# Sparse attention and a gated FFN: block transposes on VectorE, with transfers between partitions, in place of TensorE transposes after the first block

## The chip, the cores and the metric

The kernel runs on one core of one Trainium2 chip. The metric is the device time of one execution in microseconds, as the median of several runs. A hardware profile of one such execution is shown below. Engines: PE is TensorE (PEld its weight loads), ACT is ScalarE, DVE is VectorE, POOL is GpSimd, and SP is SyncE, which issues all DMAs of this kernel.

## What is computed

```python
B, H, S, D = 8, 8, 576, 64
scores = q @ k.transpose(0, 1, 3, 2) / np.sqrt(D)
rel = pos[:, None] - pos[None, :]
mask_local   = (rel >= 0) & (rel < 32)                         # heads 0 to 3
mask_strided = (rel >= 0) & (pos[None, :] % 32 == pos[:, None] % 32)   # heads 4 to 7
attn = softmax(np.where(mask, scores, -1e9))
x = (attn @ v).transpose(0, 2, 1, 3).reshape(4608, 512)
h = x @ w_in                       # 512 -> 2048
out = (h * sigmoid(h)) @ w_out     # 2048 -> 512
```

All arrays are float32. The masks make the attention sparse: a local head needs, for 32 queries, 64 keys; a strided head needs, for each of 32 residues, the 18 positions of that residue.

## The kernel before

**FFN.** The 4608 tokens are worked through in 9 blocks of 512 tokens. A block has 16 chunks `fc` of 128 of the 2048 hidden channels. For a chunk, `hidden` (L525) makes 12 matmuls of 128x512, then `silu` makes the gated value from it (tanh on ACT at L535; the product at L539, the rounded high half at L547 and the low half at L551, all on DVE), and `output` (L571) makes 12 matmuls of 128x512 with the chunk before (`lag`). Each factor is split into a high and a low float32r half, and three products of halves stand for one. When a block is done, `store` copies the four output banks `po` to `osb` on ACT (L579; two `osb` buffers) and sends them to memory (L581).

**Attention.** Heads go in pairs on the 128 partitions. For one batch of 576 tokens there are six groups: three local ones (12 tiles of 32 queries each) and three strided ones (8, 8 and 6 tiles of three residues, 54 queries each). A group passes these steps:

- `scores` (L384): small matmuls into two PSUM banks; `peak` (L402 on DVE, L408 on ACT): masking, row maximum and exponential, into the tile `sm`; `total` (L428, L429) and, for strided groups, `scale` (L432).
- `turn` (L438): one 128x128 PE transpose for each 128 columns of `sm`, three or four in a group; `turned` (L442): ACT copies the bank to `pt`.
- `values` (L455 local, L460 strided): `pt` times V. A strided result is copied by ACT to the token tile `xb` (`sorted`, L484). A local one is divided on DVE (`share`, L471) into `xq`, turned back by three PE transposes (`back`, L491) and copied by ACT to `xb` (`done`, L496).
- `x_high` (ACT, L513) and `x_low` (DVE, L517) split `xb` into the FFN's input halves `xhi` and `xlo`.

**Order.** The first batch, and the first block of the FFN, are put in order by a planner (`Steps`) with a cost for each step. From block 1 to block 6 the attention of one batch is laid into one FFN block by hand: `between` is called after the `output` of each chunk, and at the chunks 0, 3, 5, 8, 11 and 13 of a block it issues a **burst**: `turn` of group c+1, `back` of c-1, `values` of c, `scores` and `total` of c+2. Local and strided groups alternate: the bursts at 0, 5 and 11 have a local group c, and those at 3, 8 and 13 a strided one. There are 36 bursts. The order on PE is that of the code; the order on the other engines after block 0, SP's among them, comes out of the tile framework's scheduler. Four PSUM banks (`ps`) are taken in turn by `hidden` and by all attention steps, and the other four are `po`.

Of the kernel before, what the change touches and what calls it, by code (L numbers as in the profile page):

```python
# [13 lines left out]
F32 = mybir.dt.float32  # L14
# [11 lines left out]
STRIDE = 32  # L26
NJ = S // STRIDE
NP = H // 2
P = 128
# [10 lines left out]

KW = 64
SEQ = 3 * NJ
QW = 448
VT = 12
KBUFS = 2
VBUFS = 2
KFIRST = 4
VFIRST = 6  # L50
XBUFS = NP + 2


AHEAD = 6
# [3 lines left out]
class Group:  # L58
    def __init__(self, local, first, count):
        self.local, self.first, self.count = local, first, count  # L60
        self.rows = STRIDE if local else KW
        self.per = P // self.rows
        self.n = count // self.per
        step = STRIDE if local else SEQ
        self.q0 = [step * t for t in range(count)]
        half = S // STRIDE
        gap = [STRIDE if local and first < half <= first + t else 0 for t in range(count)]
        self.k0 = [q0 + g for q0, g in zip(self.q0, gap)]
        self.nq = self.q0[-1] + self.rows
        self.nk = self.k0[-1] + KW  # L70

        self.starts = [
            tuple(t % self.per for t in range(c * self.per, (c + 1) * self.per)
                  if local and (first + t) % half == 0)
            for c in range(self.n)
        ]

# [3 lines left out]
NG = len(GROUPS)  # L81
# [112 lines left out]
def sparse_attention_ffn(ctx: ExitStack, tc: tile.TileContext, kqt, vt, w_in, w_out, out):  # L194
    nc = tc.nc
# [3 lines left out]
    att = ctx.enter_context(tc.tile_pool(name="att", bufs=2))  # L199
# [31 lines left out]
    def keep(m, p0, rows, shape, steps, base, channel):  # L231
        part = m[p0 : p0 + rows, : math.prod(shape)]
        nc.gpsimd.affine_select(
            out=part, in_=part, pattern=[[s, c] for s, c in zip(steps, shape)],
            base=base, channel_multiplier=channel, compare_op=ALU.is_ge, fill=NEG,
        )

    masks = {}
    m = mask("mask_local")
    for t in range(P // STRIDE):  # L240
        keep(m, t * STRIDE, STRIDE, [KW], [1], -1, -1)
        keep(m, t * STRIDE, STRIDE, [KW], [-1], STRIDE, 1)
    masks[True, ()] = m
    for starts in sorted({s for g in GROUPS for s in g.starts if s}):
        first = const.tile([P, 72], F32, name="mask_first" + "".join(map(str, starts)))
        nc.gpsimd.tensor_copy(out=first, in_=m)
        for t in starts:
            keep(first, t * STRIDE, STRIDE, [KW], [1], -STRIDE, 0)
        masks[True, starts] = first
    m = mask("mask_strided")  # L250
    for t in range(P // KW):
        keep(m, t * KW, KW, [4, NJ], [-NJ, -1], 0, 1)
        keep(m, t * KW, KW, [4, NJ], [NJ, 0], NJ - 1, -1)
    masks[False, ()] = m
    const.tile([P, 96], F32, name="pad1")

# [35 lines left out]
    copy = {"DVE": nc.vector.tensor_copy, "ACT": nc.scalar.copy}  # L292
# [55 lines left out]
    def place_of(b):  # L348
        if b not in xs:
            xs[b] = xp.tile([P, NP, S], F32, name="xb")  # L350
        return xs[b]

    class Attention:


        def __init__(self, b, at):
            self.b, self.at, self.gi = b, at, order_of(b)[at]
            self.g = g = GROUPS[self.gi]
            self.kbd, self.vbd = kbds[kbd_of(b, at)], vbds[vbd_of(b, at)]
            self.cols = g.n * P  # L360
            self.tiles = [
                (t, t // g.per, slice(t % g.per * g.rows, (t % g.per + 1) * g.rows))
                for t in range(g.count)
            ]

            self.quick = NG * b + at < 2 * NG + 2
# [11 lines left out]
        def scores(self):  # L378
            g, kbd = self.g, self.kbd
            self.pss = [self.bank("pss") for _ in range(2)]  # L380
            for t, c, rows in self.tiles:
                for h in range(2):
                    at = slice(h * D, (h + 1) * D)
                    nc.tensor.matmul(  # L384
                        self.pss[h][rows, c * KW : (c + 1) * KW],
                        kbd[at, 1, g.q0[t] : g.q0[t] + g.rows],
                        kbd[at, 0, g.k0[t] : g.k0[t] + KW], start=True, stop=True,
                    )
# [33 lines left out]
        def total(self):  # L422
            rsum = self.rsum
            if self.quick:
                nc.vector.tensor_reduce(
                    out=rsum, in_=self.s_sb, op=ALU.add, axis=mybir.AxisListType.X
                )
            nc.vector.tensor_scalar_add(rsum, rsum, 1e-9)  # L428
            nc.vector.reciprocal(rsum, rsum)  # L429
# [4 lines left out]
        def turn(self):  # L434
            self.psp = self.bank("psp")
            for c in range(self.g.n):
                at = slice(c * P, (c + 1) * P)
                nc.tensor.transpose(self.psp[:, at], self.sm[:, at], ident)  # L438

        def turned(self, engine="ACT"):  # L440
            self.pt = att.tile([P, 512], F32, name="pt")
            copy[engine](out=self.pt[:, : self.cols], in_=self.psp[:, : self.cols])  # L442

        def values(self):
            g, pt, vbd = self.g, self.pt, self.vbd
            if g.local:
                self.pso = [self.bank("pso") for _ in range(2)]
            else:
                self.pso = self.bank("pso")
            for t, c, rows in self.tiles:  # L450
                p0 = c * P + rows.start
                for h in range(2):
                    at = slice(h * KW, (h + 1) * KW)
                    if g.local:
                        nc.tensor.matmul(  # L455
                            self.pso[h][rows, c * D : (c + 1) * D],
                            pt[at, p0 : p0 + g.rows], vbd[at, t], start=True, stop=True,
                        )
                    else:
                        nc.tensor.matmul(  # L460
                            self.pso[h * D : (h + 1) * D, t * SEQ : (t + 1) * SEQ], vbd[at, t],
                            pt[at, p0 : p0 + SEQ], start=True, stop=True,
                        )

        def share(self):
            g = self.g
            self.xq = att.tile([P, 3 * P], F32, name="xq", bufs=1)
            o_sb = self.xq.rearrange("p (c h d) -> p c h d", h=2, d=D)[:, : g.n]
            for h, o_ps in enumerate(self.halves(self.pso)):
                inv = self.rsum[:, :, h].unsqueeze(2).broadcast_to([P, g.n, D])  # L470
                nc.vector.tensor_mul(o_sb[:, :, h], o_ps, inv)  # L471
# [15 lines left out]
        def back(self):  # L487
            self.psx = self.bank("psp")
            for c in range(self.g.n):
                at = slice(c * P, (c + 1) * P)  # L490
                nc.tensor.transpose(self.psx[:, at], self.xq[:, at], ident)  # L491

        def done(self, engine="ACT"):
            flat = place_of(self.b).rearrange("p n s -> p (n s)")
            x0 = self.g.first * STRIDE
            copy[engine](out=flat[:, x0 : x0 + self.cols], in_=self.psx[:, : self.cols])  # L496

    def new_x():
        return [[None] * NP for _ in range(2)]
# [83 lines left out]
    groups = [Attention(b, at) for b in range(B) for at in range(NG)]  # L583
# [160 lines left out]
    scored, weighed = set(range(2 * NG + 2)), set(range(2 * NG))  # L744

    def load_due():

        while due:
            kind, j = due[0]
            bufs, load_one, read = (KBUFS, load_qk, scored) if kind == "k" else (  # L750
                VBUFS, load_v, weighed)
            if j - bufs not in read:
                return
            load_one(groups[j])
            due.pop(0)

    def scores(c):  # L760
        if c < len(groups):
            groups[c].scores()
            scored.add(c)
            load_due()
            groups[c].peak()

    def total(c):
        if c < len(groups):
            groups[c].total()
            if not groups[c].g.local:  # L770
                groups[c].scale()

    def turn(c):
        if c < len(groups):
            groups[c].turn()
            groups[c].turned()

    def values(c):
        if c < len(groups):
            groups[c].values()  # L780
            weighed.add(c)
            load_due()
            (groups[c].share if groups[c].g.local else groups[c].sorted)()

    def back(c):
        if groups[c].g.local:
            groups[c].back()
            groups[c].done()

    plan = {}  # L790
    for c in range(2 * NG, len(groups)):
        b, at = divmod(c, NG)
        plan[b - 1, (0, 3, 5, 8, 11, 13)[at]] = c

    def between(k, fc):
        if (k, fc) in plan:
            c = plan[k, fc]
            turn(c + 1)
            back(c - 1)
            values(c)  # L800
            scores(c + 2)
            total(c + 2)

    load_due()
    lag = (0, NFC - 1, state["g", NFC - 1])
    po = state["po"]
# [82 lines left out]
```

## Time and profile before

| | us |
|---|---|
| median of 3 runs | 921.07 (920.71 to 922.52) |
| profiled execution | 923.33 |
| its span | 921.5 (1.8 outside the span) |
| PE busy | 904.5 (98%) |
| DVE busy | 436.6 (47%) |
| ACT busy | 315.1 (34%) |
| DMA, mean throughput | 68 GB/s |
| granted PE clock, mean | 0.998 |

The span falls into three parts. Up to about 144 us the first batch's attention, the weights and block 0 are worked on; from 144 to about 744 us six blocks of 100 us each hold the 36 bursts; the last two blocks hold only FFN, with 16 chunks of 24 matmuls. A busy PE says little by itself, since its matmuls overlap: two matmuls of 128x512 that follow each other start 0.227 us apart, while each is recorded with 0.39 us. What a step costs PE is therefore read from the distance of the starts.

### The profile page before, as it was taken

How to read it: one execution, taken by the hardware profiler on the slowest of the kernel's cores; microseconds unless marked ns; L12 is line 12 of the kernel's file. 1: busy time of each engine (PE TensorE's matmuls, PEld its weight loads, DVE VectorE, ACT ScalarE, POOL GpSimd, SP SyncE). 2: the span in 40 equal slices, each digit the busy share in tenths (PEclk: the TensorE clock that was granted, in tenths of full speed). 3: DMA queues.
4: the chain of work that ended last, by engine and by line, in shares of the span. 5: the costliest groups of instructions: out<-in, count | busy, mean ns of one | idle time of the engine just before them, and what ended most of it. 6: DMA issues, size and time to landing. Idle time of an engine off the chain costs nothing.

```text
span 921.5 us, 18028 instructions
## 1 busy us (share of the span) xinstructions
PE 904.5 (98%) x7451; PEld 742.9 (81%) x7451; DVE 436.6 (47%) x1408; ACT 315.1 (34%) x897; POOL 19.0 (2%) x38
## 2 busy tenths in 40 slices
PE   8999998999999999999999999999999999999997
PEld 6777776888888888888888888888888888888886
DVE  6999665434534444434444353444443333333332
ACT  3877453422532243224342252234332221112112
POOL 4100000000000000000000000000000000000000
PEclk9999999999999999999999999999999999999999
DMA  9674533201301102112220131120210010001001
GB/s 336 217 244 155 161 101 102 64 29 38 114 27 41 63 32 91 54 29 69 83 63 30 39 101 40 37 66 32 87 40 9 1 46 1 1 1 46 1 1 46
DMA packets 34962, 63.04 MB, mean 68 GB/s; under 512 B 2624, under 2 KB 22080, under 8 KB 34880
## 3 DMA queue, kind: packets, MB, share of 16 engines
q1 hardware_dynamic: 34880, 61.89, 20.3%
q8 instruction: 58, 0.95, 0.4%
q14 instruction: 24, 0.20, 0.1%
HBM read 52.45 MB, written 9.44 MB: 67 GB/s over the span
## 4 chain that ended last, share of the span: by engine, by line
PE 87%; DVE 7%; DMA 3%; ACT 2%; issue 0%; ACTq 0%; SPq 0%
PE ps L525 39%; PE po L571 39%; PE ps L384 3%; PE ps L460 2%; DMA stage<-w_in 2%; PE ps L438 1%; PE ps L455 1%; DVE stage L287 1%; DVE w L327 1%; DVE glo L551 1%; DVE sm L402 1%; PE ps L491 1%; DMA stage<-w_out 1%; DVE th L539 1%; PE ps L639 1%; ACT stage L276 1%
## 5 line engine op out<-in xcount | busy, mean ns | idle before, releaser
L525 PE MATMUL ps<-xhi,w 128*128 128x512 f32 x1152 | 386.6, 395 | 2.2 <-DVE th L539 1.5
L525 PEld LDWEIGHTS ps<-xhi,w 128*128 128x128 f32 x1152 | 216.2, 188 | 50.5 <-DVE th L539 1.9
L539 DVE SCALAR_TENSOR_TENSOR th<-th,ps 128x512 f32<-128x512 f32 (+1 forms) x147 | 99.3, 675 | 319.2 <-ACT th L535 319.1
L535 ACT ACTIVATE th<-ps 128x512 f32<-128x512 f32 (+1 forms) x147 | 86.3, 587 | 430.0 <-PE ps L525 427.7
L525 PE MATMUL ps<-xlo,w 128*128 128x512 f32 x576 | 225.2, 391 | 1.7 <-DVE xlo L517 1.7
L571 PE MATMUL po<-w,ghi 128*128 128x512 f32 x504 | 155.4, 390 | 0.7 <-ACT ghi L547 0.7
L525 PEld LDWEIGHTS ps<-xlo,w 128*128 128x128 f32 x576 | 108.2, 188 | 23.8 <-DVE xlo L517 3.0
L571 PEld LDWEIGHTS po<-w,ghi 128*128 128x128 f32 x504 | 94.4, 188 | 20.4 <-ACT ghi L547 0.8
L551 DVE TENSOR_TENSOR glo<-th,ghi 128x512 fp32r<-128x512 f32 (+1 forms) x147 | 100.3, 682 | 12.2 <-ACT ghi L547 1.6
L571 PE MATMUL po<-w,glo 128*128 128x512 f32 x252 | 98.3, 390 | 0.3 <-DVE glo L551 0.3
L571 PE MATMUL po<-stage,ghi 128*128 128x512 f32 x288 | 88.7, 389 | 0.0
L408 ACT ACTIVATE sm<-sm,sums 128x64 f32<-128x64 f32 x226 | 75.5, 336 | 13.2 <-DVE sums L402 12.6
L571 PE MATMUL po<-v,ghi 128*128 128x512 f32 x216 | 66.7, 390 | 0.0
L571 PEld LDWEIGHTS po<-stage,ghi 128*128 128x128 f32 x288 | 54.1, 188 | 11.3
L547 DVE CAST ghi<-th 128x512 fp32r<-128x512 f32 (+1 forms) x137 | 57.7, 421 | 10.4
L571 PEld LDWEIGHTS po<-w,glo 128*128 128x128 f32 x252 | 47.3, 188 | 11.0 <-DVE glo L551 1.2
L571 PE MATMUL po<-stage,glo 128*128 128x512 f32 x144 | 56.1, 389 | 0.0
L442 ACT COPY pt<-ps 128x384 f32<-128x384 f32 (+1 forms) x40 | 20.6, 514 | 79.8 <-PE ps L438 79.8
L571 PEld LDWEIGHTS po<-v,ghi 128*128 128x128 f32 x216 | 40.4, 188 | 8.5 <-ACT ghi L547 0.2
L571 PE MATMUL po<-k,ghi 128*128 128x512 f32 x144 | 44.3, 389 | 0.0
L571 PE MATMUL po<-v,glo 128*128 128x512 f32 x108 | 42.2, 391 | 0.4 <-DVE glo L551 0.4
L408 ACT ACTIVATION_READ_ACCUMULATOR sm<-sm,sums 128x1 f32 x226 | 42.6, 188 | 0.0
(77 smaller groups left out, 737.1 us busy)
## 6 DMA issues: line engine op xcount, KB each, us to landing
v<-vt SPq DMA_DIRECT2D x24, 384.0 KB, 3.6
out<-osb SPq DMA_DIRECT2D x36, 256.0 KB, 2.0
stage<-w_in SPq DMA_DIRECT2D x16, 512.0 KB, 4.8
stage<-w_out SPq DMA_DIRECT2D x16, 512.0 KB, 3.6
k<-kqt SPq DMA_DIRECT2D x16, 442.0 KB, 4.0
k<-kqt SPq DMA_DIRECT2D x16, 416.0 KB, 4.6
v<-vt SPq DMA_DIRECT2D x16, 256.0 KB, 2.8
k<-kqt SPq DMA_DIRECT2D x8, 448.0 KB, 4.2
```

Source lines behind the costliest of these rows:

```text
L276: nc.scalar.activation(out=value, in_=value, func=AF.Prelu, scale=2.0**-112, alpha=-(2.0**32))
L287: nc.vector.scalar_tensor_tensor(out=upper, in0=upper, scalar=3, in1=lower, op0=ALU.logical_shift_left, op1=ALU.bitwise_or,)
L384: nc.tensor.matmul(self.pss[h][rows, c * KW : (c + 1) * KW], kbd[at, 1, g.q0[t] : g.q0[t] + g.rows], kbd[at, 0, g.k0[t] : g.k0[t] + KW], s ...
L408: nc.scalar.activation(out=s_sb[:, c, h], in_=s_sb[:, c, h], func=AF.Exp, bias=peaks[:, c, h : h + 1], scale=-1.0, accum_out=rsum[:, c, h ...
L442: copy[engine](out=self.pt[:, : self.cols], in_=self.psp[:, : self.cols])
L460: nc.tensor.matmul(self.pso[h * D : (h + 1) * D, t * SEQ : (t + 1) * SEQ], vbd[at, t], pt[at, p0 : p0 + SEQ], start=True, stop=True,)
L525: nc.tensor.matmul(ph, weight(0, wi, fc)[:, cc * P : (cc + 1) * P], x[xi][cc], start=(cc, n) == (0, 0), stop=(cc, n) == (NP - 1, 2),)
L535: nc.scalar.activation(out=th[:, cols], in_=ph[:, cols], func=AF.Tanh, scale=0.5)
L539: nc.vector.scalar_tensor_tensor(out=th[:, cols], in0=th[:, cols], scalar=1.0, in1=ph[:, cols], op0=ALU.add, op1=ALU.mult,)
L547: copy[engine](out=g[0][:, cols], in_=th[:, cols])
L551: nc.vector.tensor_sub(out=g[1][:, cols], in0=th[:, cols], in1=g[0][:, cols].bitcast(F32))
L571: nc.tensor.matmul(po[tt], g[gi][:, cols], weight(1, wi, fc), start=fc == 0 and n == 0, stop=fc == NFC - 1 and n == 2,)
```

## The change

After block 0 no group is turned by PE any more. `turn_by_blocks` follows `scale` (or `total`) in the same burst as the scores: one VectorE instruction transposes each 32x32 block of `sm` where it lies, into another `sm` buffer, and 16 DMAs from SP then move the 16 parts (32 partitions by 96 or 128 columns) to the partitions where `pt` needs them. `back_by_blocks` does the same from `xq` to `xb`, right after `share`, so that `back` and `done` are gone too. Group 13, whose scores belong to block 0, is turned this way between block 0 and block 1; group 12 is still turned on PE by the planner. The 128 rows of a bank are dealt to tiles in another order (`at`), so strided queries lie as two halves of 27 in 32 columns each, and the strided loads of q and k have up to 512 columns in place of 442. `xq` gets two buffers, the `sm` ring stays at three, and the `xhi` and `xlo` rings go from 6 to 5.

```diff
-QW = 448
+QW = 512
+HALF = SEQ // 2
-XBUFS = NP + 2
+XBUFS = NP + 1
...
+        self.at = [(t % self.n, t // self.n) for t in range(count)]
...
+        def blocks(self, name, bufs, src, dst):
+            n, size = self.g.n, P // STRIDE
+            mid = att.tile([P, 512 if name == "sm" else 3 * P], F32, name=name, bufs=bufs)
+            mid = mid[:, : self.cols]
+            nc.vector.transpose(
+                out=mid.rearrange("p (j c q) -> p c j q", j=size, q=STRIDE),
+                in_=src.rearrange("p (c j k) -> p c j k", j=size, k=STRIDE),
+            )
+            part = n * STRIDE
+            for r, j in itertools.product(range(size), range(size)):
+                nc.sync.dma_start(
+                    out=dst[j * STRIDE : (j + 1) * STRIDE, r * part : (r + 1) * part],
+                    in_=mid[r * STRIDE : (r + 1) * STRIDE, j * part : (j + 1) * part],
+                )
+
+        def turn_by_blocks(self):
+            pt = att.tile([P, 512], F32, name="pt")[:, : self.cols]
+            self.blocks("sm", 3, self.sm[:, : self.cols], pt)
+            self.pt = pt.rearrange("k (r c q) -> k c r q", r=P // STRIDE, q=STRIDE)
+
+        def back_by_blocks(self):
+            flat = place_of(self.b).rearrange("p n s -> p (n s)")
+            x0 = self.g.first * STRIDE
+            self.blocks("xq", 2, self.xq, flat[:, x0 : x0 + self.cols])
...
-                            pt[at, p0 : p0 + SEQ], start=True, stop=True,
+                            pt[at, c, r : r + 2, :HALF], start=True, stop=True,
...
-            self.xq = att.tile([P, 3 * P], F32, name="xq", bufs=1)
+            self.xq = att.tile([P, 3 * P], F32, name="xq", bufs=2)
...
     def scores(c):
         if c < len(groups):
             groups[c].scores()
             scored.add(c)
             load_due()
             groups[c].peak()
-
-    def total(c):
-        if c < len(groups):
             groups[c].total()
             if not groups[c].g.local:
                 groups[c].scale()
-
-    def turn(c):
-        if c < len(groups):
-            groups[c].turn()
-            groups[c].turned()
+            groups[c].turn_by_blocks()
 
     def values(c):
-        if c < len(groups):
-            groups[c].values()
-            weighed.add(c)
-            load_due()
-            (groups[c].share if groups[c].g.local else groups[c].sorted)()
-
-    def back(c):
+        groups[c].values()
+        weighed.add(c)
+        load_due()
         if groups[c].g.local:
-            groups[c].back()
-            groups[c].done()
+            groups[c].share()
+            groups[c].back_by_blocks()
+        else:
+            groups[c].sorted()
...
     def between(k, fc):
         if (k, fc) in plan:
-            c = plan[k, fc]
-            turn(c + 1)
-            back(c - 1)
-            values(c)
-            scores(c + 2)
-            total(c + 2)
-
+            values(plan[k, fc])
+            scores(plan[k, fc] + 2)
+
+    groups[2 * NG + 1].turn_by_blocks()
     load_due()
```

On PE, a strided burst (chunk 3 or 8) before, from the last matmul of `output` to the first of `hidden`:

```order
L571 MATMUL po<-w_0_701,glo 128x512
L438 MATMUL ps<-ident,sm 128x128 x3
L491 MATMUL ps<-ident,xq 128x128 x3
L460 MATMUL ps<-pt,v_77 64x54 x16
L384 MATMUL ps<-k_81 64x64 x12
L525 MATMUL ps<-xhi,w_0_616 128x512
```

The six transposes at its start are those of the groups c+1 and c-1. In the changed kernel a local burst (chunk 0, 5 or 11) begins directly with `values` (now L486), and its first eight matmuls stand so:

```order
L486 MATMUL ps<-v_77,pt 32x64 [waits DMAHW5_49,DMAHW7_49,DMAHW0_49,PE_49]
L486 MATMUL ps<-v_77,pt 32x64 [waits DMAHW2_49,DMAHW1_49]
L486 MATMUL ps<-v_77,pt 32x64 x4
L486 MATMUL ps<-v_77,pt 32x64 [waits DMAHW4_49,DMAHW3_49]
L486 MATMUL ps<-v_77,pt 32x64 [waits DMAHW6_49,DMAHW5_49]
```

The names DMAHW0 to DMAHW7 are the eight semaphores that SP's DMAs take in turn. No transpose is left, and of each six matmuls the first two wait for two transfers each (eight of the 24 do, in the places 1, 2, 7, 8, 13, 14, 19 and 20). One row here is two matmul records in the trace.

On ACT, at the end of a block (from chunk 0's tanh on, blocks 2 to 6) before:

```order
L535 ACTIVATE th<-ps 128x512 [waits DVE_49,PE_49]
L579 ACTIVATE osb<-po 128x512 [waits DMAHW0_49,PE_49]
L579 ACTIVATE osb<-po 128x512 [waits DMAHW1_49,PE_49]
L442 COPY pt<-ps 128x512 [waits PE_49]
L579 ACTIVATE osb<-po 128x512 [waits DMAHW6_49,Activation_49]
L579 ACTIVATE osb<-po 128x512 [waits DMAHW7_49,Activation_49]
L408 ACTIVATE sm,sums<-sm,sums 128x64 [waits DVE_49] x6
L535 ACTIVATE th<-ps 128x512 [waits PE_49] x2
```

and at the same place now:

```order
L570 ACTIVATE th<-ps 128x512 [waits DVE_49,PE_49]
L614 ACTIVATE osb<-po 128x512 [waits PE_49] x2
L411 ACTIVATE sm,sums<-sm,sums 128x64 [waits DVE_49,Activation_49]
L411 ACTIVATE sm,sums<-sm,sums 128x64 [waits DVE_49] x5
L570 ACTIVATE th<-ps 128x512 [waits PE_49]
L614 ACTIVATE osb<-po 128x512 [waits DMAHW5_49,Activation_49]
L614 ACTIVATE osb<-po 128x512 [waits DMAHW6_49,Activation_49]
L570 ACTIVATE th<-ps 128x512 [waits PE_49]
```

The third and fourth copy of the finished block's output banks have moved behind the six exponentials of the burst and behind chunk 1's tanh.

On SP, at the same place now (before, no transfer but those of `osb`, V, k and q stood here):

```order
L616 DMA out<-osb 128x512 [waits DMAHW5_49,Activation_49]
L616 DMA out<-osb 128x512 [waits DMAHW6_49,Activation_49]
L348 DMA v_77<-vt 128x768 [waits DMAHW7_49,PE_49]
L344 DMA k_81<-kqt 128x1024 [waits DMAHW0_49]
L460 DMA xb<-xq 32x96 [waits DMAHW1_49,DVE_49]
L616 DMA out<-osb 128x512 [waits DMAHW2_49,Activation_49]
L460 DMA xb<-xq 32x96 [waits DMAHW3_49]
L616 DMA out<-osb 128x512 [waits DMAHW4_49,Activation_49]
```

Fourteen more transfers from `xq` to `xb` and the sixteen from `sm` to `pt` follow. Each DMA waits for the one issued eight places ahead of it, and fourteen of the transfers to `xb` now stand behind the stores.

More of the change, by code (lines that the diff above doesn't have):

```diff
@@ L63, in __init__ @@
         self.n = count // self.per
-        step = STRIDE if local else SEQ
-        self.q0 = [step * t for t in range(count)]
+        self.q0 = [self.rows * t for t in range(count)]
         half = S // STRIDE
         gap = [STRIDE if local and first < half <= first + t else 0 for t in range(count)]
-        self.k0 = [q0 + g for q0, g in zip(self.q0, gap)]
+        self.k0 = [(STRIDE if local else SEQ) * t + g for t, g in enumerate(gap)]
         self.nq = self.q0[-1] + self.rows
         self.nk = self.k0[-1] + KW
+        self.at = [(t % self.n, t // self.n) for t in range(count)]
         self.starts = [
-            tuple(t % self.per for t in range(c * self.per, (c + 1) * self.per)
-                  if local and (first + t) % half == 0)
+            tuple(r for t, (at, r) in enumerate(self.at)
+                  if at == c and local and (first + t) % half == 0)
             for c in range(self.n)
@@ L250, in sparse_attention_ffn @@
     m = mask("mask_strided")
-    for t in range(P // KW):
-        keep(m, t * KW, KW, [4, NJ], [-NJ, -1], 0, 1)
-        keep(m, t * KW, KW, [4, NJ], [NJ, 0], NJ - 1, -1)
+    for t in range(P // STRIDE):
+        q0 = t % 2 * HALF
+        keep(m, t * STRIDE, STRIDE, [4, NJ], [-NJ, -1], q0, 1)
+        keep(m, t * STRIDE, STRIDE, [4, NJ], [NJ, 0], NJ - 1 - q0, -1)
     masks[False, ()] = m
@@ L361, in __init__ @@
             self.tiles = [
-                (t, t // g.per, slice(t % g.per * g.rows, (t % g.per + 1) * g.rows))
-                for t in range(g.count)
+                (t, c, slice(r * g.rows, (r + 1) * g.rows)) for t, (c, r) in enumerate(g.at)
             ]
@@ L440, in turned @@
         def turned(self, engine="ACT"):
-            self.pt = att.tile([P, 512], F32, name="pt")
-            copy[engine](out=self.pt[:, : self.cols], in_=self.psp[:, : self.cols])
+            pt = att.tile([P, 512], F32, name="pt")
+            copy[engine](out=pt[:, : self.cols], in_=self.psp[:, : self.cols])
+            self.pt = pt[:, : self.cols].rearrange("k (c r q) -> k c r q", r=P // STRIDE, q=STRIDE)
+        def blocks(self, name, bufs, src, dst):
[20 more added lines that the diff above has]
+            self.blocks("xq", 2, self.xq, flat[:, x0 : x0 + self.cols])
         def values(self):
@@ L450, in values @@
             for t, c, rows in self.tiles:
-                p0 = c * P + rows.start
+                r = rows.start // STRIDE
                 for h in range(2):
@@ L456, in values @@
                             self.pso[h][rows, c * D : (c + 1) * D],
-                            pt[at, p0 : p0 + g.rows], vbd[at, t], start=True, stop=True,
+                            pt[at, c, r], vbd[at, t], start=True, stop=True,
                         )
@@ L495, in done @@
             x0 = self.g.first * STRIDE
-            copy[engine](out=flat[:, x0 : x0 + self.cols], in_=self.psx[:, : self.cols])
+            dst = flat[:, x0 : x0 + self.cols].rearrange(
+                "p (r c q) -> p c r q", c=self.g.n, q=STRIDE
+            )
+            src = self.psx[:, : self.cols].rearrange("p (c r q) -> p c r q", c=self.g.n, q=STRIDE)
+            copy[engine](out=dst, in_=src)
     def new_x():
@@ L851 @@
             for i in range(STRIDE if g.local else SEQ):
-                q_from[gi, g.q0[t] + i] = place(g.local, g.first + t, i)
+                at = i if g.local else i // HALF * STRIDE + i % HALF
+                q_from[gi, g.q0[t] + at] = place(g.local, g.first + t, i)
             for i in range(KW if g.local else SEQ):
```

## The prediction, made before the changed kernel ran

> **What bounds the kernel now.** I read the page first: the busy shares, and the chain of work that ended last with its shares by engine.
>
> ```profile
> span 921.5 us, 18028 instructions
> PE 904.5 (98%) x7451; PEld 742.9 (81%) x7451; DVE 436.6 (47%) x1408; ACT 315.1 (34%) x897; POOL 19.0 (2%) x38
> PE 87%; DVE 7%; DMA 3%; ACT 2%; issue 0%; ACTq 0%; SPq 0%
> ```
>
> Then busy time by stage: start and end in us, length, busy time of PE, PEld, DVE, ACT and POOL (instructions in brackets), granted PE clock, DMA share, GB/s.
>
> ```profile
> 0.00:144.00 144.00, 134.02 (x1515) 105.88 (x1516) 114.97 (x391) 84.54 (x154) 19.01 (x38) 0.99 0.59 197
> 344.00:444.00 100.00, 100.00 (x879) 82.79 (x878) 44.05 (x157) 34.79 (x122) 0.00 (x0) 1.00 0.18 56
> ```
>
> A block of the middle part has PE busy for all of its 100 us at full clock; VectorE and ScalarE are idle for more than half of it, and the DMA engines work a fifth of it. So in that part what leaves PE shortens the time, and what VectorE and DMA gain is paid only where PE comes to wait for it. The FFN's matmuls stay; the change can act only in the 36 bursts, at the block ends and in the first 144 us. What it takes from PE is seen in the groups of instructions from 141 to 741 us (count, busy time, mean ns of one, idle before):
>
> ```profile
> L438 PE MATMUL ps<-ident,sm 128*128 128x128 f32 x117 | 18.4, 271 | 1.8 <-DVE sm L432 1.8
> L491 PE MATMUL ps<-ident,xq 128*128 128x128 f32 x54 | 8.8, 272 | 0.0
> ```
>
> That is 171 transposes. Their 271 ns overlap, so I priced them from the weight loads' starts, on the timeline of one strided burst:
>
> ```profile
> 364.34 0.19 PEld L571 LDWEIGHTS po<-w,glo 128*128 128x128 f32 x1
> 364.56 0.48 PEld L438 LDWEIGHTS ps<-ident,sm 128*128 128x128 f32 x3
> 365.01 0.36 PEld L491 LDWEIGHTS ps<-ident,xq 128*128 128x128 f32 x3
> 365.53 0.95 PEld L460 LDWEIGHTS ps<-pt,v 64*64 64x64 f32 x30 [0.17 <-issue]
> 367.08 0.19 PEld L525 LDWEIGHTS ps<-xhi,w 128*128 128x128 f32 x1
> ```
>
> one local burst, and one whose group has three transposes (last row):
>
> ```profile
> 377.64 0.19 PEld L571 LDWEIGHTS po<-w,glo 128*128 128x128 f32 x1
> 378.62 0.56 PEld L455 LDWEIGHTS ps<-v,pt 64*32 64x32 f32 x48 [0.17 <-PE ps L438]
> 379.12 0.80 PEld L384 LDWEIGHTS ps<-k 64*32 64x32 f32 x48
> 380.01 0.19 PEld L525 LDWEIGHTS ps<-xhi,w 128*128 128x128 f32 x1
> 416.05 0.69 PEld L384 LDWEIGHTS ps<-k 64*32 64x32 f32 x48
> ```
>
> and the same turns from FFN to small tiles in block 0, where no transposes stand between:
>
> ```profile
> 59.82 0.19 PEld L571 LDWEIGHTS po<-w,glo 128*128 128x128 f32 x1
> 60.36 0.56 PEld L455 LDWEIGHTS ps<-v,pt 64*32 64x32 f32 x48 [0.35 <-issue]
> 119.58 0.19 PEld L525 LDWEIGHTS ps<-xhi,w 128*128 128x128 f32 x1
> 120.13 0.78 PEld L460 LDWEIGHTS ps<-pt,v 64*64 64x64 f32 x24 [0.36 <-issue]
> ```
>
> **The change, term by term.**
>
> (a) *Transposes gone.* From the last FFN load to `values` takes 365.53 - 364.34 = 1.19 us with six transposes, 378.62 - 377.64 = 0.98 with four, 0.54 and 0.55 with none. So six are worth 0.65 and four 0.44: 0.109 us each, and the switch to small tiles stays. 171 x 0.109 = **-18.6 us**.
>
> By the Trainium skill's page "VectorE: DVE Perf Modes", section "The three transpose paths", a 128x128 transpose of bf16 takes 390 ns on TensorE and 311 ns on VectorE, and its "Rules for kernel authors" choose TensorE where PSUM will do as destination. With 390 ns as the price of each, 171 would bring 66.7 us in place of 18.6; the starts 0.109 us apart speak against it as a price in a stream, and those rules speak against the move itself.
>
> (b) *A wait for a PSUM bank gone.* With four transposes in a local burst the row of scores spans 0.80 us, with three 0.69; the second bank of scores was then still the one that ACT copied to `pt`. Without that bank: 11 bursts x 0.11 = **-1.2 us**.
>
> (c) *The stall before block 1 gone.* Group 13's turn waits for its own softmax:
>
> ```profile
> 143.99 0.19 PEld L571 LDWEIGHTS po<-stage,glo 128*128 128x128 f32 x1
> 146.41 0.42 PEld L438 LDWEIGHTS ps<-ident,sm 128*128 128x128 f32 x4 [2.23 <-ACT osb L579]
> 146.44 0.63 PE L438 MATMUL ps<-ident,sm 128*128 128x128 f32 x4 [1.84 <-DVE sm L432]
> ```
>
> Now group 13's `pt` is needed only at chunk 3, over 20 us on. **-2.2 us** (the idle time before the row). What is late next there is `values` of group 12, whose `pt` the planner made earlier.
>
> (d) *Waits that PE gains.* A matmul can wait for one semaphore; each further one is an instruction on PE's sequencer:
>
> ```profile
> L438 PEldq EVENT_SEMAPHORE  x1: 51/51/51, 374.0 to 374.0; - x1
> L384 PEldq EVENT_SEMAPHORE  x1: 51/51/51, 379.0 to 379.0; - x1
> ```
>
> 51 ns each. The built programs have 122 of them on PE before and 373 now, 251 more; from 0 to 251 x 0.051 = 12.8 us is possible. The sequencer's lead over the array decides: the first row is for a transpose that begins at 377.9, a lead of some 17 matmul records; the second, amid small local tiles, is only 0.1 us ahead of its matmul at 379.12. In a strided burst the waits come while that lead still stands; in a local one those at the places 13, 14, 19 and 20 come when it has been eaten. I charge 4 x 0.051 x 18 local bursts = **+3.7 us**.
>
> (e) *Block ends.* The output banks of a finished block must be copied before the next block's `output` uses them:
>
> ```profile
> 446.15 0.39 PE L571 MATMUL po<-stage,glo 128*128 128x512 f32 x1
> 447.50 1.09 ACT L579 ACTIVATE osb<-po 128x512 f32<-128x512 f32 x2
> 448.65 0.35 ACT L408 ACTIVATE sm<-sm,sums 128x64 f32<-128x64 f32 x1
> 450.56 0.19 ACT L408 ACTIVATION_READ_ACCUMULATOR sm<-sm,sums 128x1 f32 x1
> 451.14 0.62 PE L571 MATMUL po<-w,ghi 128*128 128x512 f32 x2
> 451.34 0.60 ACT L535 ACTIVATE th<-ps 128x512 f32<-128x512 f32 x1 [0.59 <-PE ps L525]
> ```
>
> Before, all four copies are done when the exponentials begin (448.65), well before `output` (451.14). Now copies three and four stand behind the exponentials and chunk 1's tanh. PE arrives earlier by a transposeless burst, so I put the tanh at 451.0 to 451.6 and the third copy's end 1.1 later, at 452.2 to 452.7, while `output` wants the third bank after six matmuls x 0.227 from about 450.8, at 452.15. That is 0.1 to 0.7 us; I take 0.35 x 5 block ends = **+1.75 us**; bounds 0 and 3.5.
>
> (f) *The start.* Strided loads grow from 442 to 512 columns and the planner lays block 0 a little differently. DMA is 0.59 busy there and PE idle for 10 of 144 us, so a little may show: **+0.5**, from -1 to +2.
>
> Sum: -18.6 - 1.2 - 2.2 + 3.7 + 1.75 + 0.5 = -16.05.
>
> **Costed at nothing, with the cover.** *VectorE* gets 53 transposes, an operation the trace lacks. The nearest rows are the passes over the same tile:
>
> ```profile
> L432 DVE TENSOR_TENSOR sm<-sm,sums 128x512 f32<-128x512 f32 x16 | 11.0, 690 | 0.4
> L432 DVE TENSOR_TENSOR sm<-sm,sums 128x384 f32<-128x384 f32 x8 | 4.4, 556 | 0.2
> ```
>
> I take 0.69 us, with twice that as the upper bound for a one-operand pass that shuffles. It stands in the burst between `scale` and the gate:
>
> ```profile
> 371.36 0.68 DVE L539 SCALAR_TENSOR_TENSOR th<-th,ps 128x512 f32<-128x512 f32 x1
> 372.54 0.69 DVE L551 TENSOR_TENSOR glo<-th,ghi 128x512 fp32r<-128x512 f32 x1
> 375.37 0.62 PE L571 MATMUL po<-w,ghi 128*128 128x512 f32 x2
> ```
>
> The gated value is whole at 373.23 and PE uses it at 375.37: 2.1 us of cover, 1.6 after PE has gained its half microsecond. A transpose over 1.6 us would delay `output` by the excess, 53 times at most. *ScalarE* loses copies and gains none. *SP and DMA* get 35 x 16 + 18 x 16 = 848 transfers. The trace has none from partition to partition; the nearest is the store of a bank:
>
> ```profile
> L581 SPq DMA_DIRECT2D out<-osb x36: 332/343/1341, 143.2 to 918.4; - x36
> DMA to landing us min/median/max: 2.0/2.0/4.9
> ```
>
> 0.33 us of issue, 2.0 us to landing. Each transfer waits for the one eight places ahead; 2.0/8 = 0.25 is less than the issue, so 0.33 is the pace, and a local burst's 32 take about 11 us and land 2 later. `pt` is wanted two bursts (27 us or more) after its scores; `xb` of the last local group of a batch, wanted for the next block's `xhi`, has 16 us. Loads and stores on the same queue come a few microseconds later, ahead of need by more than that. At the lower end (2.0 us) landing costs nothing; the upper is below, among the rivals.
>
> **Against the medians.** The profiled execution took 923.3 us, 1.8 of it outside the span and 2.3 over the median of 921.07. 923.3 - 16.05 = 907.3, and against the median **905.0 us**.
>
> **The rivals.** *Waits of PE all exposed* (faster still): every gained semaphore instruction is paid, term (d) 12.8 instead of 3.7, with (e) at 3.5: 905 + 9.1 + 1.75 = 916. For it speaks that in a local burst the lead is down to 0.1 us; against it that only eight of its 24 `values` and few other instructions have gained any. *Waits and block ends all hidden* (better): (d) and (e) at 0: 899.5. For it: the load at 120.13 shows a 0.36 us gap in which a sequencer can catch up. *VectorE late*: a transpose of 1.8 us, and the third bank held to its bound: 53 x 0.2 + 1.75 over 905 = about 917; with 1.6 us or less, none of it. *The transfers become the bound* (slower): a block has 6 x 16 + 3 x 16 = 144 of them beside some 17 others at 0.33 us. With a price p for each, 144 p + 5.6 exceeds PE's 97 us a block from p = 0.64 on, and at p = 0.66 the 100 us of before are reached. That would need a landing of 8 x 0.66 = 5.3 us with eight in flight; the longest store took 4.9, the median 2.0, the issue 0.33. At p = 1.0 a block takes 150 us: 905 + 6 x 53 = 1223. One after another at 2.0 us each, a block would take 294: 905 + 6 x 197 = 2087.
>
> The Trainium skill's page "DMA: Bandwidth & Descriptors", section "Rules for kernel authors", speaks for this rival: it advises joining many small transfers, since under 64 KB one pays mostly overhead. These have 12 to 16 KB. The trace's stores agree that 2.0 us is a floor to landing, but not that transfers queue up by it; no run here shows eight small ones in flight.
>
> **How the numbers follow.** Forecast 0.63 (own range 901 to 910); PE's waits exposed 0.09; VectorE late 0.09; all hidden 0.10; transfers the bound 0.07; 0.02 for PE gains given back in small pieces, no change. The range of 898 to 916 takes in the first four of these by their bounds; cut at both ends to what holds eight in ten, it is 899 to 913. A measurement tells no change within 0.2% (919.2 to 922.9). Faster: 0.63 + 0.09 + 0.09 + 0.10 = 0.91; same 0.02; slower 0.07.
>
> **What the profile after would show.** (a) No 128x128 matmul from a `sm` or `xq` tile after 144 us; last FFN load to `values` 0.55 us in both kinds of burst; blocks of about 97.3 us. (b) Scores 0.69 in every local burst. (c) No idle PE of 2 us at the first burst. (d) Semaphore instructions of 51 ns in front of `values`, local bursts 0.2 us longer than transposes and (b) alone give. (e) PE idle 0.1 to 0.7 us, released by an `osb` copy, in chunk 1 of blocks 2 to 6. VectorE transposes of at most 1.4 us; transfers issued every 0.33 us and landed in 2 to 3. I would be wrong if SP's transfers came further apart than 0.6 us, if `values` waited for a DMA, or if the first 144 us grew by more than 2.

## The result: slower, because the queue of SP became the bound

The changed kernel took 962.94 us (median of 4 runs, 961.16 to 964.17), the kernel before 921.74 us in the same comparison: a ratio of 1.0446, 95% interval 1.0425 to 1.0468. The forecast was 905 us, range 899 to 913. The rival named "the transfers become the bound" is what happened, at a chance of 0.07.

The profiled execution took 963.5 us. Its page:

```profile
span 961.7 us, 19172 instructions
PE 919.2 (96%) x7300; PEld 753.1 (78%) x7300; DVE 458.9 (48%) x1459; ACT 292.6 (30%) x846; POOL 19.6 (2%) x42
PE 74%; SPq 12%; DVE 6%; DMA 4%; ACT 2%; issue 2%; ACTq 0%; DVEq 0%
```

PE has 151 instructions fewer and is busy 14.7 us longer, and it idles for 42.5 us in place of 17. In the chain that ended last, SP's queue has gone from nothing to 12%, and PE has fallen from 87 to 74%. The window that was shown of before:

```profile
344.00:444.00 100.00, 94.96 (x775) 77.80 (x775) 45.38 (x148) 27.76 (x97) 0.00 (x0) 0.98 0.26 76
```

PE is no longer busy throughout, its clock is below 1, and the DMA engines are still only a quarter busy. So it isn't bytes. The two kinds of new transfers, and what the queue did to others, by source line (count, issue time min/median/max in ns, first and last start; microseconds to landing):

```profile
L460 SPq DMA_DIRECT2D pt<-sm x560: 507/589/1802, 149.6 to 757.4; - x187
L460 SPq DMA_DIRECT2D xb<-xq x288: 507/589/1774, 148.8 to 768.0; - x144
DMA to landing us min/median/max: 1.7/1.8/5.4
L348 SPq DMA_DIRECT2D v<-vt x48: 328/526/1415, 2.8 to 747.3; - x48
```

They land fast (1.8 us), but each holds SP's sequencer for 0.589 us (the median; the mean is 0.617), and the next starts 0.044 us later: one in 0.633 us, where 0.33 had been reckoned. Summed over the trace, from 148.9 to 768.6 us the 848 transfers take 523 us of issue, 84 loads and stores among them 45 us, and the gaps 52 us. Between 200 and 690 us SP is idle for 3.8 us altogether, beyond these gaps. A block, 99.9 us before, now takes 107.1 (four blocks' first bursts, 249.46 to 677.85): SP sets it. The timeline of SP at one block end, with runs of equal issues merged:

```profile
438.99 0.53 SPq L348 DMA_DIRECT2D v<-vt  x1
439.56 0.43 SPq L344 DMA_DIRECT2D k<-kqt  x1
440.09 10.82 SPq L460 DMA_DIRECT2D xb<-xq  x16
451.01 10.03 SPq L460 DMA_DIRECT2D pt<-sm  x16
461.14 1.31 SPq L348 DMA_DIRECT2D v<-vt  x1
462.49 0.61 SPq L344 DMA_DIRECT2D k<-kqt  x1
463.20 10.05 SPq L460 DMA_DIRECT2D pt<-sm  x16
473.34 1.00 SPq L616 DMA_DIRECT2D out<-osb  x2
```

The load of q and k at 462.49 had 32 transfers of earlier bursts just ahead of it, and the two stores at 473.34, whose copies ACT had made by 463.1, waited for sixteen more. PE's side of the same moment (weight loads; the bracket is the idle time before the row and what ended it):

```profile
463.69 1.00 PEld L486 LDWEIGHTS ps<-v,pt 64*32 64x32 f32 x48 [0.35 <-issue]
466.85 0.81 PEld L387 LDWEIGHTS ps<-k 64*32 64x32 f32 x48 [2.16 <-DMA k<-kqt]
476.26 0.30 PEld L606 LDWEIGHTS po<-w,ghi 128*128 128x128 f32 x2 [2.96 <-ACT osb L614]
```

Scores wait for the late load; then `output` waits for its third bank, whose copy waits for an `osb` buffer, whose store stands in SP's queue. After the first of these two waits the granted clock of PE is low for a while (0.59); after the second, which is longer, it stays at 1.00. The windows with the first wait and behind it, and with the second and behind it (the last columns are granted clock, DMA share and GB/s):

```profile
463.60:467.70 4.10, 2.10 (x97) 1.81 (x96) 1.32 (x4) 0.00 (x0) 0.00 (x0) 1.00 0.57 175
467.70:471.90 4.20, 4.20 (x16) 3.28 (x12) 1.78 (x15) 2.10 (x12) 0.00 (x0) 0.59 0.09 24
473.40:476.20 2.80, 0.34 (x2) 0.00 (x0) 1.43 (x3) 0.58 (x1) 0.00 (x0) 1.00 0.71 247
478.20:483.00 4.80, 4.80 (x23) 3.96 (x22) 0.69 (x1) 0.60 (x1) 0.00 (x0) 1.00 0.47 169
```

Where the 40.2 us went, from the starts of the weight loads of both traces (to PE's last load, 915.7 and 955.9):

| part | us |
|---|---|
| up to the first burst | +0.4 |
| all 36 bursts, without their waits (the first went from 4.39 to 2.12) | -9.6 |
| the third burst, whose `values` waited for transfers to `pt` | +5.1 |
| five bursts that waited for q and k | +10.9 |
| five times `output` at a block end, waiting for a bank | +24.8 |
| chunks at a low clock, small rest | +8.6 |

The third burst is the one place where PE waited for the new transfers themselves. Its `values` (from 176.0 us) waited four times for `pt`, whose sixteen transfers SP had issued only from 169.8 to 179.3 us, behind 32 other transfers. In the list of waits (us in all, times, longest; one of the six for q and k lies in the first 144 us):

```profile
PEld ps L486 <- DMA pt<-sm: 4.0, 4, 1.2
PEld ps L387 <- DMA k<-kqt: 10.5, 6, 2.8
```

### The profile page after: what moved, and what is told of

Its sections match the earlier page's. It is cut to its first block, busy times and chain, and to the rows that moved or that the text cites. A ratio compares the mean times of both kernels' runs of the same rounds, so it can differ in the third digit from the quotient of the medians.

```text
span 961.7 us, 19172 instructions
## 1 busy us (share of the span) xinstructions
PE 919.2 (96%) x7300; PEld 753.1 (78%) x7300; DVE 458.9 (48%) x1459; ACT 292.6 (30%) x846; POOL 19.6 (2%) x42
## 4 chain that ended last, share of the span: by engine, by line
PE 74%; SPq 12%; DVE 6%; DMA 4%; ACT 2%; issue 2%; ACTq 0%; DVEq 0%
PE ps L560 34%; PE po L606 33%; SPq L460 12%; PE ps L387 3%; PE ps L491 2%; DMA out<-osb 1%; PE ps L486 1%; DVE stage L291 1%; DMA stage<-w_in 1%; DVE w L331 1%; DVE th L574 1%; DMA stage<-w_out 1%; PE ps L674 1%; DVE glo L586 1%; ACT osb L614 1%
## 5 line engine op out<-in xcount | busy, mean ns | idle before, releaser
L560 PE MATMUL ps<-xhi,w 128*128 128x512 f32 x1152 | 392.0, 400 | 1.3 <-DVE th L574 1.2
L560 PEld LDWEIGHTS ps<-xhi,w 128*128 128x128 f32 x1152 | 220.0, 191 | 51.6 <-DVE th L574 1.4
L606 PE MATMUL po<-w,ghi 128*128 128x512 f32 x504 | 159.4, 398 | 19.6 <-ACT osb L614 19.6
L560 PEld LDWEIGHTS ps<-xlo,w 128*128 128x128 f32 x576 | 110.6, 192 | 21.8
L387 PE MATMUL ps<-k 64*32 64x64 f32 (+1 forms) x1856 | 49.7, 234 | 9.4 <-DMA k<-kqt 9.3
L387 PEld LDWEIGHTS ps<-k 64*32 64x32 f32 (+1 forms) x1856 | 42.2, 124 | 13.7 <-DMA k<-kqt 10.5
```

Of the source, the lines that this page charges most:

```text
L387: nc.tensor.matmul(self.pss[h][rows, c * KW : (c + 1) * KW], kbd[at, 1, g.q0[t] : g.q0[t] + g.rows], kbd[at, 0, g.k0[t] : g.k0[t] + KW], s ...
L560: nc.tensor.matmul(ph, weight(0, wi, fc)[:, cc * P : (cc + 1) * P], x[xi][cc], start=(cc, n) == (0, 0), stop=(cc, n) == (NP - 1, 2),)
L606: nc.tensor.matmul(po[tt], g[gi][:, cols], weight(1, wi, fc), start=fc == 0 and n == 0, stop=fc == NFC - 1 and n == 2,)
```

## The experiments

Two theories of the 49 us of stalls and low clock. *The queue is the bound*: SP needs more time for a block than PE, and whatever PE waits for is the queue in another dress. *The place in the queue*: SP would have time enough, but loads and stores stand behind sixteen transfers at a bad moment. A third question was why the bursts, without their waits, had gained 9.6 us in place of the 18.3 of the terms (a) to (d).

**What an issue costs (`issue_cost`).** Behind some chunks of the block after the last burst, eight transfers of one kind:

```
+ q.dma_start(out=b[to, c], in_=a[lo, c])          # 32x128, tile to tile; SP, ACT, POOL
+ q.dma_start(out=b[:, c], in_=a[:, c])            # 128x128, tile to tile
+ q.dma_start(out=b[lo, c], in_=flat[lo, c])       # 32x128 from memory
+ q.dma_start(out=b[:, c], in_=flat[:P, c])        # 128x128 from memory
```

> The changed kernel, with transfers added in the block after the last burst, where the queue of SP is idle: eight in a row of one kind behind each of several chunks (32x128 and 32x96 from tile to tile as in the change, 128x128 and two of 128x512 from tile to tile, 32x128 and 128x128 from memory, and 32x128 from tile to tile issued by ACT and by POOL). The time itself should be that of the changed kernel within 2 us. If a transfer's price on SP is its kind (both ends on chip), the 32x128 ones keep the 0.59 us of issue and 0.63 us of spacing that they have in the bursts, even on an idle queue, and those from memory cost 0.33. If the price comes from the pressure of a full queue (each waits for the one eight places ahead), the first eight here cost 0.33 each. If it is the number of rows, 128x128 costs about four times 32x128 or 128x128 from memory as much as that from a tile.

It took 963.94 us. By source line:

```profile
L837 SPq DMA_DIRECT2D k<-k x8: 534/582/590, 769.5 to 773.9; - x8
L837 ACTq DMA_DIRECT2D k<-k x8: 515/577/613, 798.6 to 803.2; - x8
L837 POOL DMA_DIRECT2D k<-k x8: 498/498/638, 801.1 to 805.4; - x8
L841 SPq DMA_DIRECT2D k<-k x8: 465/599/604, 779.6 to 786.3; - x8
L843 SPq DMA_DIRECT2D k<-kqt x8: 419/420/1006, 787.6 to 791.9; - x8
L845 SPq DMA_DIRECT2D k<-kqt x8: 422/430/432, 792.4 to 795.7; - x8
```

128 rows cost what 32 do (0.599 and 0.582 us from tile to tile; 0.430 and 0.420 from memory), so neither size nor rows make the price here. It differs by the ends of the transfer: tile to tile 0.58 to 0.60, memory to tile 0.42 to 0.43, where 0.33 was expected, and tile to memory (the stores of before) 0.34. The ends are not all: the loads of q and k took 0.546 us in the kernel before, those of V 0.339. And SP's queue was not idle, as the expectation had it: the first of these transfers began 0.1 us behind the last one to `xb`. The idle case stands in the trace of `xb_pool` (below). After 200 us, the 20 transfers to `pt` there that began after a pause of more than 2 us took 0.511 to 0.523 us, and those that followed without a pause had a median of 0.589. So most of the price is there without a full queue.

**Fewer transfers (`diag`, `diag2`, `diag1`).** Four of each sixteen blocks stay on their partitions; POOL copies four, two or one of them:

```diff
-            for r, j in itertools.product(range(size), range(size)):
+            for j in range(size):          # diag2: range(2); diag1: range(1); the rest stay DMAs
+                rows, cols = slice(j * STRIDE, (j + 1) * STRIDE), slice(j * part, (j + 1) * part)
+                nc.gpsimd.tensor_copy(out=dst[rows, cols], in_=mid[rows, cols])
+            for r, j in itertools.permutations(range(size), 2):
                 nc.sync.dma_start(
```

> The changed kernel with the four blocks of each sixteen that stay on their partitions copied by POOL, so that SP issues 12 transfers in place of 16 (36 fewer a block). Theory 'SP's queue is the bound': a block of SP shrinks from 106 to 106 - 36 x 0.633 = 83 us, below PE's 98 to 99; the stalls at the block ends (16 us on loads, 25 us on output banks, 8 us of half clock) go, 912 to 916 us. Rival 'the place in the queue': the stores still stand behind twelve transfers in place of sixteen; a quarter of the stalls goes, about 950 us.

> As diag, with two of the four blocks copied by POOL: 14 transfers, 18 fewer a block. Theory 'SP's queue is the bound': SP needs 95.0 us a block, PE 98.6, so the knee is passed and PE is the bound: 914 us as with all four, up to 918 where the transfers of the close bursts (chunks 11, 13 and 0) still pile up. Rival 'each transfer has its price on the path': half way from 963 to 914, 938 us.

> As diag, but POOL copies only one of the four blocks that stay on their partitions: SP issues 15 transfers for each transpose, 9 fewer a block. Theory 'SP's queue is the bound, 0.633 us each': a block of SP takes 106.4 - 5.7 = 100.7 us, still above PE's 98.6, so nearly the whole price of 53 transfers shows: 963 - 33.5 = 929 us (926 to 932). Rival 'the place in the queue': a sixteenth of the stalls at the block ends, 960 us.

| transfers of a transpose | time, us | ratio to before (95%) |
|---|---|---|
| 16 (the change) | 962.94 | 1.0446 (1.0425 to 1.0468) |
| 15 (`diag1`) | 932.27 | 1.0101 (1.0084 to 1.0118) |
| 14 (`diag2`) | 917.27 | 0.9937 (0.9923 to 0.9952) |
| 12 (`diag`) | 914.06 | 0.9906 (0.9891 to 0.9921) |

The first 53 transfers taken away bring 30.7 us, 0.58 us each; the next 53 bring 15.0, the last 106 only 3.2. That is a bound with a knee, and it lies where SP's time for a block meets PE's. `diag1` came out 0.3 us above the range expected, the other two inside theirs. The chain that ended last of `diag1` (7% on SP's queue) and of `diag` (2%):

```profile
PE 79%; SPq 7%; DVE 6%; DMA 4%; ACT 3%; issue 1%; ACTq 0%; DVEq 0%
```

```profile
PE 87%; DVE 5%; DMA 3%; SPq 2%; ACT 2%; issue 1%; ACTq 0%
```

In `diag` the stores still stand behind twelve transfers, but SP is idle for 19% of the time from 200 to 690 us, and no wait of PE for an output bank is left. So the place in the queue hurt where the queue never emptied.

**Stores from another queue (`stores_act`).**

```diff
-            nc.sync.dma_start(out=out[r0 : r0 + P, :], in_=osb)
+            nc.scalar.dma_start(out=out[r0 : r0 + P, :], in_=osb)
```

> The changed kernel with the 36 stores of the output banks issued from ACT's queue in place of SP's. Theory 'SP's queue is the bound': SP is relieved of 24 issues of about 0.5 us in the stretch, so 950 us; the wait of PE moves from the output banks to the loads of q and k. Rival 'the place in the queue': only the stores behind sixteen transfers hurt; the waits for output banks vanish (24.8 us) and with them about half of the slow-clock time (4 us), 934 us.

953.29 us (ratio 1.0332, 1.0316 to 1.0347). The wait for output banks is gone, and PE waits for loads instead; its longest waits in the changed kernel (us in all, times, longest), and here:

```profile
PE po L606 <- ACT osb L614: 19.6, 5, 5.0
PE ps L387 <- DMA k<-kqt: 9.3, 6, 2.6
```

```profile
PE ps L387 <- DMA k<-kqt: 21.7, 10, 3.3
```

Where PE waited moved. The 9.7 us gained are near what SP was relieved of: 20 stores stood in its full stretch (24 were reckoned), at half a microsecond each.

**The same transfers from other queues (`xb_pool`, `xb_act`).** The 288 to `xb` alone:

```diff
-                nc.sync.dma_start(
+                (nc.sync if name == "sm" else nc.gpsimd).dma_start(     # xb_act: nc.scalar
```

> The changed kernel with all its transfers kept, but the 288 to xb (48 a block) issued from POOL's queue, which is otherwise empty after block 0. Theory 'the issue on SP's queue is the bound': SP has 106.4 - 48 x 0.633 = 76 us a block, PE 98.6, the time is that of diag, 914 us (912 to 918). Rival 'the transfers themselves or the DMA engines are the bound, whoever issues them': 960 us or more.

> The same 288 transfers issued from ACT's queue. Only SP's relief counted, this would be 914 us too. But sixteen issues in a row at 0.6 us stand on ACT ahead of a tanh that PE's next output needs: 9.7 us, of which about 5 us are covered by a hidden and an output; 18 local bursts x 4 to 6 us, with the half clock after each wait, give 990 to 1030 us.

`xb_pool`: 913.61 us (0.9897, 0.9880 to 0.9914), as `diag`, with every transfer still made, and in the bursts PE waits for no load, no output bank and no transfer. The bound was SP's issuing, not the DMA engines. The Trainium skill, page "DMA: Bandwidth & Descriptors", section "Rules for kernel authors", says that spreading DMAs over several queues only saves issue time of the sequencer; the trace agrees, and here that time was the bound.

`xb_act`: 1095.52 us (1.1863, 1.1840 to 1.1886), far beyond what was expected. ACT's timeline in one local burst, and from the list of waits PE's wait for the gated value in the whole run (us in all, times, longest):

```profile
364.98 9.58 ACTq L460 DMA_DIRECT2D xb<-xq  x15
374.66 0.35 ACT L411 ACTIVATE sm<-sm,sums 128x64 f32<-128x64 f32 x1 [14.67 <-DMA xb<-xq]
376.67 1.05 ACT L570 ACTIVATE th<-ps 128x512 f32<-128x512 f32 x2
```

```profile
PE po L606 <- DVE ghi L582: 137.3, 18, 9.7
```

The sixteen issues hold up the six exponentials, and two tanh stand behind those: 9.6 + 2 us before the first tanh starts, 18 waits of up to 9.7 us, and a mean granted clock of 0.924. The expectation had put only the issues ahead of the tanh.

**The order of the tiles (`order_only`, `before_order`, `diag_order`).** The change deals tiles to the rows of a bank in another way, and so neighbours in PE's order now lie on the same rows. `order_only` sorts them back; `before_order` puts the changed order into the kernel before (`key=lambda tile: (tile[2].start, tile[1])`):

```diff
                 (t, c, slice(r * g.rows, (r + 1) * g.rows)) for t, (c, r) in enumerate(g.at)
             ]
+            self.tiles.sort(key=lambda tile: (tile[1], tile[2].start))
```

> The changed kernel with one thing undone: the small matmuls of scores and values go through the tiles in the order of before (neighbours in the order on different rows of the bank). Theory 'SP's queue is the bound' (SP issues without a break from 147 to 769 us): PE only waits longer, no change, 961 to 965 us, although bursts get shorter by about 0.3 us each. Rival 'PE's bursts are part of the path': 30 undisturbed bursts by 0.25 to 0.3 us, 954 us.

> The kernel before with one part of the change alone: the small matmuls of scores and values go through the tiles in the changed kernel's order (neighbours on the same rows of the bank). PE is the bound there. If that order makes the small matmuls run one after another, bursts grow by the 2.4 us a block seen between diag and order_only, and the first batch a little: 922 + 14 = 936 us. Rival 'the order is neutral, the bursts of the changed kernel were longer by waits for transfers': 922 us.

> diag together with order_only: 12 transfers, and the tiles in the order of before. With SP's queue below PE's time a shorter burst now counts. The bursts of order_only that were not disturbed are shorter than those of diag by 0.54 (local, 1.72 against 2.27) and 0.30, 0.18, 0.30 us (strided), 2.4 us a block: 914 - 6 x 2.4 = 900 us (898 to 902). Rival 'the order of the tiles does not matter, the waits of PE do': 912 to 914 us.

`order_only` took 958.24 us (1.0379, 1.0358 to 1.0401): between the two expectations. In its trace SP's stretch from first to last transfer is 620.8 us, against 619.7 in the changed kernel, so there the theory held; PE ends 2.2 us earlier because the work behind the last burst begins earlier. The median's other 2.5 us stay open (its four runs spread over 5 us).

`before_order` took 932.99 us (1.0115, 1.0099 to 1.0132): the order alone costs 10 us where PE is the bound (14 were expected), 9.2 of them in the bursts. `diag_order` took 899.79 us (0.9756, 0.9738 to 0.9773), the best of all. One local burst's weight loads in the changed kernel, and in `diag_order`, from its first one to the first of `hidden` (the rows between are left out):

```profile
396.15 0.89 PEld L486 LDWEIGHTS ps<-v,pt 64*32 64x32 f32 x45 [0.35 <-issue]
397.87 0.19 PEld L560 LDWEIGHTS ps<-xhi,w 128*128 128x128 f32 x1
```

```profile
367.81 0.55 PEld L490 LDWEIGHTS ps<-v,pt 64*32 64x32 f32 x47 [0.35 <-issue]
368.96 0.19 PEld L564 LDWEIGHTS ps<-xhi,w 128*128 128x128 f32 x1
```

The same 96 small matmuls take 1.72 us with neighbours on the same rows and 1.15 with neighbours on different ones. That the order does this is shown; why it does is not.

## Why the prediction was wrong, step by step

**The step that failed** is the one on SP, costed at nothing: "0.33 us of issue ... so 0.33 is the pace". It measured 0.589 of issue, one in 0.633. The store of a bank was taken as the nearest row, because no transfer from tile to tile was in the trace. But another row of the same trace had the loads of q and k at 0.546 us of issue:

```profile
L340 SPq DMA_DIRECT2D k<-kqt x48: 327/546/1306, 0.7 to 667.1; - x48
```

A bound from both sides, as for the other unknown costs, would have run from 0.33 to 0.55, plus the 0.04 between issues. 144 x 0.59 is 85 us of a 97 us block before any other issue: the rival next to the forecast, not 7 in 100. Its threshold (0.64 to 0.66) was also set too high, for it put the 17 others at 0.33, where they measured 0.53, and left out the gaps. With 14 others a block (84 in six) at 0.53 and a gap of 0.04 behind each issue, PE's 97 us are full at 0.57 us a transfer. The landing was right: 1.8 us, against 2.0. And the cover named for late loads and stores, "ahead of need by more than that", held for a queue that empties between bursts, which this one did not. Two of the three signs of being wrong came: transfers 0.633 us apart, and `values` that waited for a DMA, in the third burst. The first 144 us grew by 0.4 us only.

**(a) and (b) Transposes and the bank: right in kind, a little small.** Where the order of tiles is undisturbed (`diag_order`), strided bursts went from 2.74, 2.63 and 2.51 to 2.08, 1.97 and 1.85, 0.65 to 0.66 each, against the 0.65 predicted. Local ones with four transposes went from 2.36 to 1.70: 0.66, a little more than 0.44 + 0.11; those with three (chunk 5) from 2.15 to 1.70: 0.45, against 0.33.

**(c) The first burst: right.** The idle 2.2 us are gone. The burst went from 4.39 to 1.90 in `diag_order` (2.12 in the changed kernel), against -2.2 and 0.44 for its four transposes.

**(d) Waits of PE: too dear.** The charge of 0.2 us for each local burst didn't show, since these came out shorter than (a) and (b) alone give.

**(e) Block ends: right place, wrong reason.** PE did wait for the third bank, but for a store in SP's queue, not for the exponentials ahead of the copy: with SP relieved (`diag`), the wait was nil.

**(f) The start:** +0.4, against +0.5.

**A step left out: the order of the small matmuls.** The new dealing of tiles was seen, and its effect on PE not priced: +9.2 us in the bursts of `before_order`, and the 14 us between `diag` and `diag_order`.

**VectorE: right.** Its transposes took what a pass over the tile takes (0.69 was reckoned for 512 columns), and the gate's cover held:

```profile
L454 DVE STREAM_TRANSPOSE sm<-sm 128x512 f32<-128x512 f32 x12 | 8.4, 701 | 0.0
L454 DVE STREAM_TRANSPOSE xq<-xq 128x384 f32<-128x384 f32 x18 | 10.4, 578 | 0.8 <-DVE xq L502 0.2
```

In all, the 36 bursts of `diag_order` are 23.9 us shorter than before. So the idea brings 2.4% (`diag_order`) once SP's queue is below PE's time and the small matmuls keep their order; as it was put, it lost 4.5%.

## What to carry to other kernels

Before moving work to DMA, multiply the number of transfers by the issue time of one, take the dearest issue on that queue and not the cheapest, add the other transfers and the gaps, and compare that with the time of the bound engine for the same stretch. A queue near that time has no slack for anything that stands in it, and the loss then shows as waits for buffers and loads at other places. When tiles are dealt anew, look at which neighbours in PE's order share rows of the bank.

## What the runs showed of the hardware that was not expected

- Issue on SP, in a row: tile to tile 0.58 to 0.60 us and memory to tile 0.42 to 0.43, with 32 rows as with 128; stores 0.34. POOL's queue took 0.50 for the same tile-to-tile transfer, ACT's 0.58.
- Loads of V, 0.328 us of issue at the least, had a median of 0.526 in the changed kernel. In `xb_pool`, after 200 us, they took 0.333 to 0.346 us after a pause of SP and mostly 0.526 or more directly behind a transfer. Why is open.
- In the window with the wait of 2.2 us at 464.7 us, where PE was busy for 2.1 of 4.1 us, the granted clock was still 1.00; it was 0.59 over the next 4.2 us, and a `hidden` took 4.2 us in place of 2.7. After the wait of 2.96 us at 473.3 us it stayed at 1.00. The Trainium skill, page "TensorE: Matmul & The Clock Gate", Part 1, speaks of one idle window of about 3.4 us as the cause. Here a shorter single wait, with small matmuls around it, was enough once, and a longer one was not, so the length of a wait alone doesn't tell.
